# Ten blocks instead of eight by seven products, the division moved from VectorE to ScalarE and GpSimd, one turning for two, quarter sums behind the last slot

## Chip, cores, metric

The kernel runs on one core of one Trainium2 chip. The metric is the device time of one execution in microseconds (us). "The profile" is one execution recorded by the hardware profiler, "the trace" its single instructions. L followed by a number is a line of the kernel that the profile belongs to, so the same statement has different numbers in different kernels.

## The reference, cut to what matters

Threshold attention over 8 batches of 8 heads, 576 positions, head size 64; its output is the input x of an MLP with exact GELU.

```python
scores = scale * np.matmul(q, k.transpose(0, 1, 3, 2))
thresh = np.max(scores, axis=-1, keepdims=True) - tau
scores = np.where(scores >= thresh, scores, -1000000000.0)
attn = np.exp(scores - np.max(scores, axis=-1, keepdims=True))
attn = attn / (np.sum(attn, axis=-1, keepdims=True) + 1e-09)
x = attn @ v                       # to (4608, 512)
h = x @ w_in                       # 512 -> 2048
g = 0.5 * h * (1.0 + erf(h / sqrt(2)))
out = g @ w_out                    # 2048 -> 512
```

## The kernel before, the parts that matter

The 4608 rows of x are 18 blocks of 256. The first ten are "plain": their matmuls fill gaps of TensorE while attention runs. The last eight go two at a time ("duos") through an algorithm with seven products of quarters instead of eight, after attention. Attention goes by 32 pairs of heads with five slots each (four of 128 query rows, and the tails of both heads). From pair 4 on, p (the unnormalized attention) is turned by VectorE in 32x32 squares and regrouped by transfers from SBUF to SBUF into pT. In slot 2 of the next pair, TensorE makes xT = v^T pT, and it is divided by the row sums, which a series of transfers has laid out as inv.

```python
def softmax_head(p, i):                # per slot
    nc.vector.tensor_reduce(nmx, sc, op=ALU.max, negate=True)
    nc.gpsimd.tensor_scalar(thr, nmx, -1.0, tau_eff, ...)
    nc.scalar.activation(w, sc, AF.Exp, bias=nmx)
def softmax_tail(p, i):
    nc.vector.scalar_tensor_tensor(row, sc, thr, row, op0=ALU.is_ge, op1=ALU.mult, accum_out=den)
def divisors(p):                       # slot 4, behind the tail
    ...
    nc.sync.dma_start(rows, turned)    # to DRAM
    ...                                # four transfers back, spread over the partitions:
    nc.sync.dma_start(inv, rows)
def regroup(p, i):
    if i == 1:
        s["pT"] = [one.tile([P, KR, S], ...) for e in range(2)]   # pool of one buffer
    for a in range(4):
        ...                            # i = 1 (in slot 2) and i = 3: columns of two slots
        for e in (1, 0):
            nc.sync.dma_start(pT[e][:, :, a*P:(a+1)*P][:, :, half], pd[e][rows, :, half])
# order of one slot
scores; softmax_head; gelus of the slot before; (slot 2: xT); softmax_tail;
divide; turn_p; divide; regroup; divisors; next(loads of q, k or v on gpsimd); turn_qk; fill
```

In the traces of this case every engine, and every queue that issues transfers, goes through its instructions in the order of the program (below, thr of slot 3 starts 0.04 us after the last load of k ahead of it).

## Time and profile before

| | kernel before |
|---|---|
| time, median of the first 3 runs | 1431.48 us (1431.28 to 1433.82) |
| xT of pair 4 starts (the "first xT") | 206.6 us |
| from there to the 5th xT (four pairs) | 117.7 us |
| xT of the 5th to the 27th pair, period | 30.55 us (324.3 to 996.4 us, 22 periods) |
| last of these xT to the second duo | 88.2 us |
| one duo | 97.5 us |

The 28 pairs with turning are counted from pair 4 on. What follows the start of the second duo is three times 97.5 us (four times after) and a rest of 52.9 us that the change leaves nearly alone (52.6 after). So the rows add up to the span, and each change of time can be booked in one of them. The 22 periods are read from the starts of xT on TensorE.

### The profile page before, as it was taken

How to read it: one execution, taken by the hardware profiler on the slowest of the kernel's cores; microseconds unless marked ns; L12 is line 12 of the kernel's file. 1: busy time of each engine (PE TensorE's matmuls, PEld its weight loads, DVE VectorE, ACT ScalarE, POOL GpSimd, SP SyncE). 2: the span in 40 equal slices, each digit the busy share in tenths (PEclk: the TensorE clock that was granted, in tenths of full speed). 3: DMA queues.
4: the chain of work that ended last, by engine and by line, in shares of the span. 5: the costliest groups of instructions: out<-in, count | busy, mean ns of one | idle time of the engine just before them, and what ended most of it. 6: DMA issues, size and time to landing. Idle time of an engine off the chain costs nothing.

```text
span 1430.0 us, 19776 instructions
## 1 busy us (share of the span) xinstructions
PE 1385.1 (97%) x6544; PEld 960.9 (67%) x6544; DVE 900.0 (63%) x1908; ACT 640.8 (45%) x1039; POOL 389.1 (27%) x810
## 2 busy tenths in 40 slices
PE   5898999999999999999999999999999999999999
PEld 4666547566466574665746657466488888888887
DVE  5887787777767777777777777777654142241230
ACT  5758525436256373562745627457142141230320
POOL 4443244433434434434434344330000000000000
PEclk8999999999999999999999999999999999999999
DMA  9977167776667776677776777765500100100000
GB/s 260 297 264 241 40 144 150 152 150 133 131 137 145 153 147 133 142 140 159 156 140 143 160 154 152 142 135 100 107 0 1 44 1 0 59 1 8 22 1 30
DMA packets 449492, 167.06 MB, mean 117 GB/s; under 512 B 413040, under 2 KB 432048, under 8 KB 449392
## 3 DMA queue, kind: packets, MB, share of 16 engines
q1 hardware_dynamic: 423184, 108.65, 38.8%
q0 software_dynamic: 23808, 56.57, 12.9%
q8 instruction: 53, 0.87, 0.2%
q10 hardware_dynamic: 2400, 0.59, 0.2%
q14 instruction: 47, 0.39, 0.1%
HBM read 71.68 MB, written 11.47 MB: 58 GB/s over the span
## 4 chain that ended last, share of the span: by engine, by line
PE 85%; DVE 6%; ACT 5%; DMA 2%; issue 1%; SPq 1%; POOL 0%; DVEq 0%; ACTq 0%; POOLq 0%
PE bank L641 27%; PE hT L520 18%; PE o_ps L532 17%; PE sc L355 12%; PE xT L460 9%; ACT p L370 2%; DVE p L386 1%; PE tr L301 1%; DVE nmx L367 1%; DVE power L185 1%; ACT L500 1%; ACT diag L400 1%; DMA pd<-in_moe_w_in_dram 1%; ACT L507 0%; DVE expo L176 0%
## 5 line engine op out<-in xcount | busy, mean ns | idle before, releaser
L370 ACT ACTIVATE p<-sc,nmx 128x576 f32<-128x576 f32 x288 | 202.5, 739 | 384.4 <-DVE nmx L367 384.4
L367 DVE TENSOR_REDUCE nmx<-sc 128x1 f32<-128x576 f32 x288 | 205.0, 749 | 149.8 <-PE sc L355 149.8
L520 PE MATMUL hT<-x,w_in 128*128 128x256 f32 x1280 | 296.2, 384 | 0.0
L532 PE MATMUL o_ps<-w_out,g 128*128 128x512 f32 x640 | 295.1, 604 | 0.0
L520 PEld LDWEIGHTS hT<-x,w_in 128*128 128x128 f32 x1280 | 238.4, 190 | 56.9 <-issue 25.2
L386 DVE SCALAR_TENSOR_TENSOR p<-sc,thr,p 128x576 f32<-128x576 f32 x288 | 225.4, 816 | 65.2 <-ACT p L370 64.2
L368 POOL TENSOR_SCALAR thr<-nmx,tau_eff 128x1 f32<-128x1 f32 x288 | 85.0, 295 | 547.4 <-DVE nmx L367 544.9
L532 PEld LDWEIGHTS o_ps<-w_out,g 128*128 128x128 f32 x640 | 117.1, 190 | 141.0 <-issue 139.2
L355 PE MATMUL sc<-kT,qT 64*128 64x288 f32 x960 | 165.0, 432 | 2.6 <-DVE p L386 2.4
L460 PE MATMUL xT<-pT,v 128*64 128x288 f32 (+2 forms) x1280 | 164.4, 409 | 3.2 <-ACT g L500 3.2
L433 DVE STREAM_TRANSPOSE pd<-p 128x576 f32<-128x576 f32 x224 | 160.8, 756 | 2.9
L355 PEld LDWEIGHTS sc<-kT,qT 64*128 64x128 f32 x960 | 92.9, 187 | 84.2 <-issue 71.8
L460 PEld LDWEIGHTS xT<-pT,v 128*64 128x64 f32 x1280 | 90.2, 137 | 73.4 <-issue 13.5
L232 POOL DMA_DIRECT2D v<-in_v_dram x208 | 111.0, 537 | 10.5 <-issue 9.5
L641 PE MATMUL bank<-x,w_in 128*128 128x256 f32 x384 | 94.7, 383 | 3.2 <-DVE x L655 3.2
L507 ACT ACT_TABLE_LOAD x71 | 91.1, 1283 | 1.3
L500 ACT ACT_TABLE_LOAD x71 | 91.1, 1283 | 1.3
L641 PE MATMUL bank<-unit 128*128 128x256 f32 x352 | 88.6, 382 | 0.0
L641 PEld LDWEIGHTS bank<-x,w_in 128*128 128x128 f32 x384 | 73.7, 192 | 14.2 <-issue 4.1
L223 POOL DMA_DIRECT2D q<-in_q_dram x104 | 70.9, 686 | 15.9 <-issue 15.0
L641 PEld LDWEIGHTS bank<-unit 128*128 128x128 f32 x352 | 67.4, 192 | 9.4
L301 PE MATMUL tr<-diag,p 128*128 128x128 f32 (+1 forms) x360 | 51.8, 312 | 22.1 <-ACT diag L400 13.8
(143 smaller groups left out, 1346.4 us busy)
## 6 DMA issues: line engine op xcount, KB each, us to landing
pT<-pd SPq DMA_DIRECT2D x448, 160.0 KB, 3.9
pT<-pd_tail SPq DMA_DIRECT2D x112, 80.0 KB, 2.8
q<-in_q_dram POOLq DMA_DIRECT2D x104, 72.0 KB, 4.0
k<-in_k_dram POOLq DMA_DIRECT2D x104, 72.0 KB, 2.6
out_dram<-o_sb SPq DMA_DIRECT2D x28, 256.0 KB, 3.9
inv<-turned SPq DMA_DIRECT2D x56, 128.0 KB, 3.9
v<-in_v_dram POOLq DMA_DIRECT2D x156, 40.0 KB, 3.0
raw<-in_moe_w_in_dram POOLq DMA_DIRECT2D x8, 512.0 KB, 5.5
```

Of the source, the lines that this page charges most:

```text
L232: eng.dma_start(t[r:P:4, e, 0:n, :], rows[:, r * KR:r * KR + n, :])
L355: nc.tensor.matmul(sc[e][:, h, 0:HALF], lhsT=lhsT, rhs=s["kT"][rows, at:at + HALF], start=True, stop=True)
L367: nc.vector.tensor_reduce(nmx[:, e:e + 1], sc, axis=AXIS.XY, op=ALU.max, negate=True)
L370: nc.scalar.activation(w[:, e * S:(e + 1) * S].rearrange("p (h s) -> p h s", h=2), sc, AF.Exp, bias=nmx[:, e:e + 1], scale=1.0)
L386: nc.vector.scalar_tensor_tensor(row, sc[e][:, :, 0:HALF], thr[:, e:e + 1], row, op0=ALU.is_ge, op1=ALU.mult, accum_out=den[e])
L433: nc.vector.transpose(to[:, 0:NB, :], w[:, e * S:(e + 1) * S].rearrange("p (b i) -> p b i", i=Q))
L460: nc.tensor.matmul(xT[f, 0:hi - lo], lhsT=s["v"][:, e, c, :], rhs=pT[:, c, lo:hi], start=(c == 0), stop=(c == KR - 1))
L500: nc.scalar.activation(t, hT, AF.Gelu)
L507: nc.scalar.activation(warm[:, 1:2], warm[:, 0:1], AF.Exp)
L520: nc.tensor.matmul(hT[:, j % 2, :], lhsT=w_in_sb[c][:, j * P:(j + 1) * P], rhs=x_blk[n][:, c, :], start=(c == 0), stop=(c == N_DM - 1))
L532: nc.tensor.matmul(o[:, 0:d_model], lhsT=g[j][:, m * P:(m + 1) * P], rhs=w_out_sb[j], start=(j == 0), stop=(j == N_DF - 1))
L641: nc.tensor.matmul(to, lhsT=l, rhs=r, start=start and k == 0, stop=k == len(pairs) - 1, skip_group_check=not start)
```

## The change

Its intent: two more blocks by seven products save an eighth of their matmul work; the smaller fill then needs shorter slots, so VectorE is relieved (division by ScalarE and GpSimd, two turnings in one); the start and the turn to the last stage lose waits.

```diff
-    PLAIN = N_BLK - 8
+    PLAIN = N_BLK - 10
-    AWAY = [PLAIN, PLAIN + 1, PLAIN + 2]
+    AWAY = list(range(PLAIN, PLAIN + 5))
+    warm = const.tile([P, 2], FP32, name="warm")      # was allocated behind the weights
+    nc.vector.memset(warm, 0.0)
     ident = const.tile([P, P], FP32, name="ident")
...
-    pd = [const.tile([P, 4 * KR, P], FP32, name=f"pd{e}") for e in range(2)]
+    turned_p = const.tile([P, 2, 4 * KR, P], FP32, name="turned_p")
+    pd = [turned_p[:, e, :, :] for e in range(2)]
...
-        for e in reversed(range(n)):                   # two turnings of 576
-            nc.vector.transpose(to[:, 0:NB, :], w[:, e * S:(e + 1) * S]...)
+        nc.vector.transpose(turned_p[:, :, 0:NB, ...], w.rearrange(...))   # one of 1152
...
-                    nc.vector.tensor_tensor(to, x, by[:, at:at + size], op=ALU.mult)
+                nc.scalar.copy(to, x)
+                if by is not None:
+                    nc.gpsimd.tensor_tensor(to, to, by[:, at:at + size], op=ALU.mult)
...                                                     # seven-product stage
+        x_sums(x_ext, *DUOS[0])                         # in weights_in, behind the last slot
-                nc.sync.dma_start(out[row:row + P, :], hi[m])
+                store(n2, m, hi[m], 0)                  # half-width stores, earlier
...
+    nc.scalar.activation(warm[:, 1:2], warm[:, 0:1], AF.Exp)    # behind load_early(0)
-        convert(3000 if n < 2 * HP else ...)
+        convert(0 if n == 0 else 3400 if n < 2 * HP else ...)
```

The multiplies now stand where xT is made, ahead of the loads of k on GpSimd.

More of the change, by code (lines that the diff above doesn't have):

```diff
@@ L67 @@
     N_BLK = B * S // TOK
-    PLAIN = N_BLK - 8
-    AWAY = [PLAIN, PLAIN + 1, PLAIN + 2]
-    order = list(range(PLAIN + 3, N_BLK)) + AWAY
+    PLAIN = N_BLK - 10
+    AWAY = list(range(PLAIN, PLAIN + 5))
+    order = list(range(PLAIN + 5, N_BLK)) + AWAY
     DUOS = list(zip(order[0::2], order[1::2]))
@@ L429, in turn_p @@
         w = s.pop(("p", i))
-        n = 1 if i == NC else 2
-        for e in reversed(range(n)):
-            to = pd_tail[p % 2] if i == NC else pd[e][:, :, i * Q:(i + 1) * Q]
-            nc.vector.transpose(to[:, 0:NB, :], w[:, e * S:(e + 1) * S].rearrange("p (b i) -> p b i", i=Q))
+        if i == NC:
+            nc.vector.transpose(pd_tail[p % 2][:, 0:NB, :], w[:, 0:S].rearrange("p (b i) -> p b i", i=Q))
+            return
+        nc.vector.transpose(
+            turned_p[:, :, 0:NB, i * Q:(i + 1) * Q], w.rearrange("p (e b i) -> p e b i", e=2, i=Q))
     def regroup(p, i):
@@ L474, in divide @@
                 to, x = x_blk[n][:, hp, o:o + size], xT[:, at - lo:at - lo + size]
-                if by is None:
-                    nc.scalar.copy(to, x)
-                else:
-                    nc.vector.tensor_tensor(to, x, by[:, at:at + size], op=ALU.mult)
+                nc.scalar.copy(to, x)
+                if by is not None:
+                    nc.gpsimd.tensor_tensor(to, to, by[:, at:at + size], op=ALU.mult)
                 at += size
-        if by is not None:
-            return divide
         divide()
@@ L491 @@
     dirty = [False]
-    warm = const.tile([P, 2], FP32, name="warm")
-    nc.vector.memset(warm, 0.0)
     def gelus(left):
@@ L512, in block_steps @@
         g = {}
+        mlp["layer"] = 1
         for j in range(N_DF):
@@ L526, in block_steps @@
             for j in range(N_DF):
+                mlp["layer"] = 2
                 yield NS_OUT, len(pieces) - N_DF + j + 1
@@ L537, in block_steps @@
             nc.sync.dma_start(out[row:row + P, :], o_sb)
-    mlp = {"n": 0, "steps": None, "next": None, "debt": 0.0}
+    mlp = {"n": 0, "steps": None, "next": None, "debt": 0.0, "layer": 0}
     def fill(ns, tokens):
@@ L584, in weights_in @@
         room += unit(work, "p", 2) + unit(work, "p", 2)
-        rest = [units(v_sb[i % 4])[0] for i in range(NP - 4, NP - 1)]
+        x_ext = [units(v_sb[i % 4])[0].rearrange("p (c t) -> p c t", c=NK) for i in range(NP - 4, NP - 1)]
         s1, s2, s4 = ({} for _ in range(3))
@@ L594, in weights_in @@
                 vec.tensor_tensor(s4[c, h], w_in_sb[NK + c][:, lo], s2[c, h], op=ALU.subtract)
-        return (s1, s2, s4), room + rest
+        assert mlp["n"] == PLAIN and mlp["layer"] == 2
+        for h in range(HF // U):
+            for c in range(NK):
+                a = w_in_sb[c][:, HF + h * U:HF + (h + 1) * U]
+                vec.tensor_tensor(a, w_in_sb[c][:, h * U:(h + 1) * U], a, op=ALU.subtract)
+        x_sums(x_ext, *DUOS[0])
+        return (s1, s2, s4), x_ext, room
     away = {}
@@ L605, in bring, with x_sums, strassen @@
         nc.sync.dma_start(x_blk[n], away.pop(n))
-    def strassen(ext, room):
+    def x_sums(x_ext, n1, n2):
+        t1, t2, t4 = x_ext
+        a, b = x_blk[n1], x_blk[n2]
+        b11, b21, b12, b22 = a[:, 0:NK, :], a[:, NK:2 * NK, :], b[:, 0:NK, :], b[:, NK:2 * NK, :]
+        vec.tensor_tensor(t1, b12, b11, op=ALU.subtract)
+        vec.tensor_tensor(t2, b22, t1, op=ALU.subtract)
+        vec.tensor_tensor(b12, b22, b12, op=ALU.subtract)
+        vec.tensor_tensor(t4, b21, t2, op=ALU.subtract)
+    def strassen(ext, x_ext, room):
         s1, s2, s4 = ext
-        for h in range(HF // U):
-            for c in range(NK):
-                a = w_in_sb[c][:, HF + h * U:HF + (h + 1) * U]
-                vec.tensor_tensor(a, w_in_sb[c][:, h * U:(h + 1) * U], a, op=ALU.subtract)
         room = room + units(v_sb[(NP - 1) % 4]) + [u for t in pd_tail for u in units(t)]
         room += [x for _ in range(2) for x in unit(xg, "x", 2)]
-        x_ext = [room.pop().rearrange("p (c t) -> p c t", c=NK) for _ in range(3)]
         o_ext = [room.pop() for _ in range(2)]
@@ L647, in bank @@
             return ps.tile([P, 512], FP32, tag="mm", name="bank")
-        def x_sums(n1, n2):
-            t1, t2, t4 = x_ext
-            a, b = x_blk[n1], x_blk[n2]
-            b11, b21, b12, b22 = a[:, 0:NK, :], a[:, NK:2 * NK, :], b[:, 0:NK, :], b[:, NK:2 * NK, :]
-            vec.tensor_tensor(t1, b12, b11, op=ALU.subtract)
-            vec.tensor_tensor(t2, b22, t1, op=ALU.subtract)
-            vec.tensor_tensor(b12, b22, b12, op=ALU.subtract)
-            vec.tensor_tensor(t4, b21, t2, op=ALU.subtract)
         def w_out_sums(j):
@@ L664, in w_out_sums, with store @@
             vec.tensor_tensor(wt4(j), b21, wt2(j), op=ALU.subtract)
+        def store(n, m, t, at):
+            row = n * TOK + m * P
+            nc.sync.dma_start(out[row:row + P, at:at + HD], t[:, at:at + HD])
         def finish_chunk(j, x, p3):
@@ L671, in finish_chunk @@
             vec.tensor_tensor(g21(j), g11(j), g21(j), op=ALU.subtract)
-        x_sums(*DUOS[0])
         for sb, (n1, n2) in enumerate(DUOS):
@@ L724, in strassen @@
                 vec.tensor_tensor(lo[m][:, 0:HD], lo[m][:, 0:HD], vs[m], op=ALU.add)
+                store(n1, m, lo[m], 0)
             for n in DUOS[sb + 1] if sb + 1 < len(DUOS) else ():
@@ L728, in strassen @@
             if sb + 1 < len(DUOS):
-                x_sums(*DUOS[sb + 1])
+                x_sums(x_ext, *DUOS[sb + 1])
             for m in ms:
@@ L742, in strassen @@
                 vec.tensor_tensor(hi[m][:, HD:2 * HD], hi[m][:, HD:2 * HD], xs[m], op=ALU.add)
-                row = n2 * TOK + m * P
-                nc.sync.dma_start(out[row:row + P, :], hi[m])
+                store(n2, m, hi[m], HD)
             for m in ms:
@@ L747, in strassen @@
                 nc.scalar.copy(lo[m][:, HD:2 * HD], xs[m])
-                row = n1 * TOK + m * P
-                nc.sync.dma_start(out[row:row + P, :], lo[m])
+                store(n1, m, lo[m], HD)
     load_early(0)
+    nc.scalar.activation(warm[:, 1:2], warm[:, 0:1], AF.Exp)
     load_early(1)
@@ L769 @@
     GOAL = [(-1, 0.0), (START - 1, 0.0), (BATCH - 1, 0.55)]
-    GOAL += [(BATCH * (m + 2) + WEIGH, x) for m, x in enumerate([1.96, 3.3, 4.64, 5.98, 7.32, 8.66, PLAIN])]
+    GOAL += [(BATCH * (m + 2) + WEIGH, x) for m, x in enumerate([1.96, 2.97, 3.98, 4.98, 5.99, 6.99, PLAIN])]
     def goal(n):
@@ L796 @@
             table()
-        made = []
         for args in due:
@@ L801 @@
         if p > EARLY and i == WEIGH:
-            made = [weigh_v(p - 1, h * HALF, (h + 1) * HALF) for h in range(2)]
+            for h in range(2):
+                weigh_v(p - 1, h * HALF, (h + 1) * HALF)
         owed += (goal(n) - goal(n - 1)) * BLK_NS * (PARTS[i] if not early and p < NP else 1.0)
@@ L811 @@
             softmax_tail(p, i)
-        if made:
-            made[0]()
         if p < NP and not early:
             turn_p(p, i)
-        if made:
-            made[1]()
         if p < NP and not early:
@@ L845 @@
             turn_qk(p + 1)
-        convert(3000 if n < 2 * HP else 3650 if n < BATCH - 1 else 1e9)
+        convert(0 if n == 0 else 3400 if n < 2 * HP else 3650 if n < BATCH - 1 else 1e9)
         if early:
```

## The prediction

> **What bounds the kernel now.** I read the page first (busy shares, then the 40 slices), then the busy time by stretch, the chain that ended last, and the timeline of single slots.
>
> ```profile
> PE 1385.1 (97%) x6544; PEld 960.9 (67%) x6544; DVE 900.0 (63%) x1908; ACT 640.8 (45%) x1039; POOL 389.1 (27%) x810
> ...
> 0.00:40.00 40.00, 24.69 (x150) 18.79 (x150) 22.66 (x56) 23.19 (x49) 18.66 (x46) 0.87 0.97 269
> 560.00:600.00 40.00, 40.00 (x184) 25.01 (x182) 30.86 (x63) 15.86 (x22) 15.81 (x33) 1.00 0.72 147
> 1000.00:1040.00 40.00, 36.77 (x131) 19.19 (x128) 23.08 (x44) 5.70 (x9) 0.88 (x3) 0.92 0.48 95
> 1120.00:1160.00 40.00, 40.00 (x187) 35.19 (x186) 9.88 (x24) 12.12 (x31) 0.00 (x0) 1.00 0.12 40
> ```
>
> The columns are PE, PEld, DVE, ACT and POOL busy, granted clock, DMA share, GB/s. TensorE is full from 200 us on, except at the turn from attention to the seven-product stage near 1030 us; the start is two thirds full. In the middle stage VectorE is already 77% busy and DMA 72%: TensorE binds there only because plain MLP blocks fill it.
>
> ```profile
> 990.85 4.49 PE o_ps L532 x10
> 996.51 5.00 PE xT L460 x40
> ...
> 1182.21 96.97 PE bank L641 x448
> 1279.68 96.97 PE bank L641 x448
> ```
>
> These pieces of the chain give the prices. One duo (two blocks by seven products) starts every 1279.68 - 1182.21 = 97.5 us. A plain block has 128 instructions of L520 and 64 of L532; longer runs in the chain grow by 0.215 us and 0.43 us an instruction, so two blocks cost 2 x (128 x 0.215 + 64 x 0.43) = 110 us at the margin.
>
> The middle stage goes by pairs of heads, in five slots each: scores, softmax, turning, then fill. Starts of consecutive xT are 30.5 us apart on average (294.75 to 996.51 us, 23 pairs). One full slot:
>
> ```profile
> 594.29 1.24 PE L355 MATMUL sc<-kT,qT 64*128 64x288 f32 x8
> 595.46 4.58 PE L520 MATMUL hT<-x,w_in 128*128 128x256 f32 x20
> 595.57 1.42 DVE L367 TENSOR_REDUCE nmx<-sc 128x1 f32<-128x576 f32 x2 [1.24 <-PE sc L355]
> 596.36 1.41 ACT L370 ACTIVATE p<-sc,nmx 128x576 f32<-128x576 f32 x2 [4.53 <-DVE nmx L367]
> 597.20 0.82 DVE L386 SCALAR_TENSOR_TENSOR p<-sc,thr,p 128x576 f32<-128x576 f32 x1 [0.21 <-ACT p L370]
> ...
> 598.80 1.44 DVE L433 STREAM_TRANSPOSE pd<-p 128x576 f32<-128x576 f32 x2
> 599.98 1.24 PE L355 MATMUL sc<-kT,qT 64*128 64x288 f32 x8
> ```
>
> TensorE's slot is 599.98 - 594.29 = 5.7 us, of which 20 fill instructions are 4.5. VectorE's round, from maximum to the end of the turning, is 600.24 - 595.57 = 4.67 us: only 1 us of slack.
>
> **What the Trainium skill says.** (1) "GPSIMD Engine Reference", Elementwise: a two-input elementwise op takes about 2.6 cycles an element at 1.2 GHz, and the engine has no PSUM access. The latter is why ScalarE must copy first. No GpSimd multiply is in this trace; even its one-element thr takes 295 ns. (2) "ScalarE: Activation LUTs", What ACT_TABLE_LOAD costs: 1283 ns a load, which the page repeats exactly (1283). The section gives 186 ns + 0.833 ns an element for an ACTIVATE with immediate scale and bias; the trace's PSUM copy of 512 takes 584 ns. (3) "VectorE: DVE Perf Modes", Side-by-side: about 150 cycles of fixed cost an instruction; the turning of 576 takes 756 ns, 156 over 576/0.96. (4) "TensorE: Matmul & The Clock Gate", What's actually happening: an idle window near 3.4 us halves the clock. The trace agrees: after a 3.23 us wait, groups of four that later take 0.86 us take 1.7.
>
> **The change, part by part.**
>
> *Two blocks move.* The fill of the last 24 of the 28 pairs shrinks from 0.335 to 0.251 block (the first four keep theirs). The fifth duo adds 97.5 us for certain. What comes off depends on how far the pair can shrink; nominally 110, net -12.7.
>
> *TensorE's new pair.* A pair's fill in L520 instructions is 0.251 x 256 = 64, shared 1.2, 1.2, 0.8, 1.2, 0.6. A full slot: scores 1.17 + 15.4 x 0.215 + 0.17 for switching = 4.67 us. Slot 2: 1.17 + 5.0 (xT) + 10.3 x 0.215 + 0.17 = 8.56. Slot 4 is too short: 2.8 us of PE work, but the next scores wait for its L386, in this trace 3.65 us after slot 4's scores started. Sum 3 x 4.67 + 8.56 + 3.67 = 26.2; with the same arithmetic for before I get 30.4 (measured 30.5). So at best 24 x 4.2 = 101 us come off, not 110.
>
> *VectorE.* Divides leave it: 112 in all, some 1.2 us a pair, but in slot 2, where it has slack. One turning of 1152 instead of two of 576 is 156 + 1200 = 1.36 us for 1.44 (estimate): its round falls to 4.6, just under TensorE's 4.67. So both are needed merely not to make VectorE the bound.
>
> *ScalarE.* Four copies a pair, 4 x 186 + 576 x 0.833 = 1.2 us, estimated from that section. A slot with one gelu takes exp 1.41 + two loads 2.57 + gelu 0.60 + gaps, about 4.75 us: on the edge, near +0.1 a slot.
>
> *GpSimd.* Four multiplies a pair of 576 columns together: 576 x 2.17 ns + 4 x 0.25 = 2.2 us (estimate from the first section and the 295 ns of thr). What matters is their place in the queue, below.
>
> *Ends.* The quarter sums stand behind the last slot, before the last pair's division, so the 3.23 us wait below and the slow clock after it (2.6 us) should go; a new wait for the last pT may give back a bit: -5. Dropping the conversions in slot 0 keeps VectorE from waiting for weights at 18 to 21 us ahead of the second slot's maximum: -3 to -4. Early table load and half-width last stores: some tenths.
>
> ```profile
> 1034.57 2.04 PE L641 MATMUL bank<-x,w_in 128*128 128x256 f32 x4 [3.23 <-DVE x L655]
> ```
>
> **The rivals.** *A: TensorE stays the bound.* Pair 26.3 us with the ScalarE edge: 1431.5 + 97.5 - 24 x (30.5 - 26.3) - 9 = 1419 us. For it: the slots were plainly sized so that 4.67 meets 4.6.
>
> *B: GpSimd's queue becomes the wait.* In the changed order GpSimd runs, in slot 2: thr, four multiplies, four loads of k, then thr of slot 3. The multiplies need inv, which comes at the end of a long DMA series:
>
> ```profile
> 584.59 8.16 SPq L448 DMA_DIRECT2D pT<-pd  x8
> ...
> 599.60 0.60 SPq L419 DMA_DIRECT2D inv<-turned  x1
> ...
> 603.00 2.69 POOL L223 DMA_DIRECT2D k<-in_k_dram  x4
> ```
>
> The series starts as slot 3 is turned (584.59), and inv's second half is issued at 599.60 and lands 4.4 us later: 19.4 us, set by DMA and not shortened. In the kernel before that is 4 us into slot 2, just when VectorE is free to divide. In the changed one slot 2 begins 2.9 us earlier relative to the series, and the joint turning starts it 0.7 later: inv lands 7.6 us into slot 2. Then multiplies 2.2, loads of k 2.7, thr 0.3: 12.9 us into slot 2. L386 of slot 3 wants thr 8.5 + 1.28 + 1.64 = 11.4 us in. So it starts 1.4 us late, the scores of slot 4 wait on it, and nothing makes up for it: pair 27.7 us, total 1431.5 + 97.5 - 24 x 2.8 - 9 = 1453 us. For it: order and durations; against it: the multiply's duration is an estimate, and whoever sized the fill would have seen such a wait.
>
> *C: DMA binds.* From the end of xT, 20 transfers at about 1 us each plus landing 2.8 and xT's second half 2.5 make a loop of 25.8 us (the pT buffer is single), while loads of k now fall among the pT transfers. The mean share would rise from 72% to about 80%. If transfers stretch by a tenth, pair 28 to 28.5, total 1460 to 1472.
>
> *D: a full gain.* If slot 4 didn't wait and the ends gave more: 1405 to 1410.
>
> **Range and chances.** The loss of slots against the certain 97.5 us leaves little gain in any rival: only D comes near 2% (under 1403). I hold B a little likelier than A by its mechanism, and A likelier than it looks because the change appears tuned; between 1419 and 1453 I put 1438, with 1412 to 1464 to take in A and the milder half of C. Faster by over 2%: 0.05; within: 0.80; slower, over 1460: 0.15.
>
> **What would show it.** The duos: five of 97.5 us. Pairs of xT 26.2 to 26.5 us apart speak for A; about 27.7, with L386 waiting for thr some 1.4 us once a pair and a like wait of scores for L386 on TensorE, for B; SP issue without gaps and xT waiting for pT, for C. The turning: one op near 1.36 us. The multiplies: near 0.5 us each; much longer or much shorter breaks B's sum. The wait of 3.23 us gone and the clock at 1.00 at the turn; the second maximum near 17 us instead of 21.57. The prediction is wrong if pairs fall below 26 us (slot 4 did not hold them) or if the fifth duo is dearer than 97.5.

## More of the kernel before

The page and the slot are shown in the prediction. One view is added: the queue of SyncE (SPq), which issues pT, turned and inv. Columns: start, duration of the issues, queue, line, transfer and count; a gap between lines is time in which nothing is issued (a line of many issues can hide short gaps inside).

```profile
600.24 0.62 SPq L421 DMA_DIRECT2D inv<-turned  x1
606.29 16.82 SPq L448 DMA_DIRECT2D pT<-pd  x16
623.21 3.44 SPq L444 DMA_DIRECT2D pT<-pd_tail  x4
626.75 0.58 SPq L413 DMA_DIRECT2D turned<-turned  x1
```

Between the last inv (600.86 us) and the first pT (606.29) this queue stands 5.4 us: it waits for xT to have read the old pT. That gap is the slack of the kernel before.

## The result, and the profile after

| | before | after | difference |
|---|---|---|---|
| time, median of 4 | 1431.38 us (1428.93 to 1433.82) | 1500.91 us (1499.34 to 1505.41) | |
| span of the profiled run | 1430.0 us | 1499.4 us | +69.4 |
| first xT | 206.6 | 209.7 | +3.1 |
| four pairs | 117.7 | 117.5 | -0.2 |
| 22 periods of xT | 22 x 30.55 | 22 x 29.43 | -24.8 |
| last of these xT to the second duo | 88.2 | 82.2 | -6.0 |
| fifth duo | | 97.5 | +97.5 |

The ratio is 1.0491 (95% interval 1.0462 to 1.052). Ratios here are the mean time of one kernel's runs over that of the other's of the same rounds, so not quite the ratio of the medians. Only the fifth duo adds much, and the pairs give too little back: the shorter fill shortened the pair by 1.1 us where 2.8 (rival B) or 4.2 (rival A) was predicted. After, in the columns of the prediction's fences: the page's busy times, the busy times by stretch, and the chain at the turn.

```profile
PE 1398.0 (93%) x6608; PEld 983.1 (66%) x6608; DVE 895.5 (60%) x1750; ACT 650.3 (43%) x1166; POOL 438.2 (29%) x922
```

```profile
0.00:40.00 40.00, 25.02 (x136) 19.31 (x137) 19.02 (x48) 22.03 (x47) 16.12 (x41) 0.94 0.97 251
560.00:600.00 40.00, 35.64 (x198) 24.54 (x198) 29.35 (x53) 29.32 (x41) 17.89 (x37) 1.00 0.78 135
1120.00:1160.00 40.00, 39.49 (x183) 34.44 (x183) 16.43 (x41) 16.14 (x41) 0.00 (x0) 1.00 0.00 1
```

```profile
974.72 5.00 PE xT L464 x40
1056.92 96.97 PE bank L652 x448
```

From 560 to 600 us TensorE has 4.4 us of idle time, which it did not have before (40.00 busy); the start and the duos look as before, and the chain has the turn at 82.2 us. VectorE is busy for 29.35 of these 40 us, where it was 30.86 before, so its load alone isn't the bound. SyncE's queue after:

```profile
593.91 0.58 SPq L416 DMA_DIRECT2D turned<-turned  x1
597.72 0.60 SPq L422 DMA_DIRECT2D inv<-turned  x1
...
600.57 17.79 SPq L452 DMA_DIRECT2D pT<-turned_p  x16
618.45 3.62 SPq L448 DMA_DIRECT2D pT<-pd_tail  x4
622.17 0.58 SPq L416 DMA_DIRECT2D turned<-turned  x1
626.00 0.59 SPq L422 DMA_DIRECT2D inv<-turned  x1
...
628.74 7.82 SPq L452 DMA_DIRECT2D pT<-turned_p  x8
636.66 2.40 SPq L537 DMA_DIRECT2D out_dram<-o_sb  x1
```

The 5.4 us of slack are gone. Two pauses are left in a round: the 3.2 us from the end of turned's issue (622.75) to the first inv (626.00), in which turned lands in DRAM, and one that the line of 16 issues hides: its ninth issue starts at 610.51, 1.9 us after the eighth has ended, since slot 3 must be turned first. From turned to turned is 622.17 - 593.91 = 28.3 us. What this queue waited for from 330 to 975 us (total us, times, longest), two lines of the kernel before, then two of the changed one:

```profile
SPq L448 <- PE xT L460: 117.5, 22, 7.1
SPq L419 <- DMA turned<-turned: 28.3, 21, 1.5
```

```profile
SPq L422 <- DMA turned<-turned: 65.2, 23, 4.3
SPq L452 <- PE xT L464: 6.1, 6, 1.3
```

So the slack, the wait for xT, was used up in the whole stage, and at the same time the queue's own round grew: without its gap it took 30.5 - 5.4 = 25.1 us before. A store of a plain block, 2.40 us, stands in the same queue and comes on top. TensorE's xT ran from 595.43 to 600.50, and the next pT is issued at 600.57: that is a second round of the same length, xT 5.1, pT 17.8, tails 3.7, landing 1.4 until the next xT at 623.49. A third goes through GpSimd. These are lines of the chain that ended last in the same pair (start, duration, what):

```profile
627.30 3.72 DMA inv<-turned
...
631.87 1.14 POOL x L481 x3
...
634.34 1.32 POOL k L226 x2
...
635.70 0.32 POOL thr L371
...
636.78 0.83 DVE p L389 x3
...
637.64 1.38 DVE turned_p L436
```

inv lands, the multiplies run, then the loads of k, then thr of slot 3, then VectorE masks and turns slot 3, without which the second half of pT and the next turned can't go. The waits after, from 330 to 975 us (engine, line, releaser: total us, times, longest):

```profile
POOL x L481 <- DMA inv<-turned: 119.3, 17, 9.6
DVE p L389 <- POOL thr L371: 51.2, 29, 3.5
PE sc L358 <- DVE p L389: 43.5, 38, 2.6
```

Before, VectorE waited 0.6 us in all for thr in this stage. So three rounds met in one pair: GpSimd's queue, SyncE's queue, and the single buffer pT. The last two are 28.1 to 28.3 us long here; the length of the first alone isn't shown. The experiments take them apart.

### The profile page after: what moved, and what is told of

The parts are those of the page before. It is cut to its first block, busy times and chain, and to the rows that moved or that the text cites. A ratio compares the mean times of both kernels' runs of the same rounds, so it can differ in the third digit from the quotient of the medians. Undisturbed runs are those within 1.5% of the kernel's fastest.

```text
span 1499.4 us, 20084 instructions
## 1 busy us (share of the span) xinstructions
PE 1398.0 (93%) x6608; PEld 983.1 (66%) x6608; DVE 895.5 (60%) x1750; ACT 650.3 (43%) x1166; POOL 438.2 (29%) x922
## 4 chain that ended last, share of the span: by engine, by line
PE 52%; DVE 12%; DMA 12%; ACT 8%; POOL 6%; issue 5%; SPq 4%; DVEq 0%; POOLq 0%; ACTq 0%
PE bank L652 32%; PE sc L358 6%; PE hT L519 5%; PE o_ps L532 5%; DMA inv<-turned 5%; DMA turned<-turned 4%; DVE p L389 4%; ACT p L373 3%; POOL k L226 3%; DVE turned_p L436 3%; PE xT L464 3%; DVE nmx L370 2%; POOL x L481 2%; DMA pT<-turned_p 1%; ACT L505 1%
## 5 line engine op out<-in xcount | busy, mean ns | idle before, releaser
L519 PE MATMUL hT<-x,w_in 128*128 128x256 f32 x1024 | 244.0, 389 | 0.0
L532 PE MATMUL o_ps<-w_out,g 128*128 128x512 f32 x512 | 238.9, 605 | 0.0
L519 PEld LDWEIGHTS hT<-x,w_in 128*128 128x128 f32 x1024 | 192.1, 192 | 52.4 <-issue 24.7
L532 PEld LDWEIGHTS o_ps<-w_out,g 128*128 128x128 f32 x512 | 92.8, 190 | 110.4 <-issue 107.7
L436 DVE STREAM_TRANSPOSE turned_p<-p 128x1152 f32<-128x1152 f32 x112 | 154.4, 1378 | 4.9 <-DMA pT<-pd_tail 1.1
L652 PE MATMUL bank<-x,w_in 128*128 128x256 f32 x480 | 116.7, 379 | 0.0
L652 PE MATMUL bank<-w_out,unit 128*128 128x256 f32 x520 | 115.5, 379 | 0.0
L652 PEld LDWEIGHTS bank<-w_out,unit 128*128 128x128 f32 x520 | 98.8, 190 | 13.4
L481 POOL TENSOR_TENSOR x<-x,inv 128x192 f32<-128x192 f32 (+7 forms) x112 | 51.3, 490 | 186.6 <-DMA inv<-turned 157.8
L652 PE MATMUL bank<-v,unit 128*128 128x256 f32 x320 | 82.1, 379 | 0.0
```

The lines of the kernel that those rows point to most:

```text
L436: nc.vector.transpose(turned_p[:, :, 0:NB, i * Q:(i + 1) * Q], w.rearrange("p (e b i) -> p e b i", e=2, i=Q))
L519: nc.tensor.matmul(hT[:, j % 2, :], lhsT=w_in_sb[c][:, j * P:(j + 1) * P], rhs=x_blk[n][:, c, :], start=(c == 0), stop=(c == N_DM - 1))
L532: nc.tensor.matmul(o[:, 0:d_model], lhsT=g[j][:, m * P:(m + 1) * P], rhs=w_out_sb[j], start=(j == 0), stop=(j == N_DF - 1))
L652: nc.tensor.matmul(to, lhsT=l, rhs=r, start=start and k == 0, stop=k == len(pairs) - 1, skip_group_check=not start)
```

## The experiments

Eighteen kernels ran, all correct. "Pair" is the mean of the 22 periods, read as above. The kernel before took 1428.3 to 1429.9 us (medians) beside them.

### Which part costs: div_dve, eight, ten

div_dve puts the old division back into the changed kernel; eight is the changed kernel with eight seven-product blocks; ten is the kernel before with ten.

```diff
 # div_dve
-                nc.scalar.copy(to, x)
-                    nc.gpsimd.tensor_tensor(to, to, by[:, at:at + size], op=ALU.mult)
+                    nc.vector.tensor_tensor(to, x, by[:, at:at + size], op=ALU.mult)
 # eight (ten is the reverse, in the kernel before; AWAY and the goals of the fill go with it)
-    PLAIN = N_BLK - 10
+    PLAIN = N_BLK - 8
```

> The changed kernel, with the division back on VectorE straight out of the accumulator, as before the change (no copies by ScalarE, no multiplies by GpSimd); ten blocks, joint turning and all else kept. Theory 1 (queue of GpSimd): VectorE now takes the wait for inv itself, in slot 2, but GpSimd is free: pair 27.5 to 28.5, time 1450 to 1478 us. Theory 2 (series of transfers): pair 29 or more, time above 1488 us. Theory 3 (VectorE's own work is the bound): the pair becomes longer than 29.4, time above 1505 us.

> The changed kernel with eight blocks by seven products and the old fill, all else kept. If the new engine placement costs only where the fill is too small to hide it (theories 1 and 2 alike), the pair stays at 30.5 us and the time is 1424 to 1440 us (6 us from the turn gained, 3 at the start lost). If the waits cost in full whatever the fill, since they stop the scores that stand ahead of the fill, the pair is 31.5 us or more and the time above 1455 us.

> The kernel before with ten blocks by seven products and the smaller fill, all else as before (divide on VectorE, two turnings, quarter sums behind the last division). Theory 1: VectorE's round and the divide set the pair, 28 to 28.5 us, time about 1428 + 97 - 24 x 2.3 = 1470 us. Theory 2 (series of transfers): pair 29.4, time 1500 us or more. If it were the old engine placement that bounds, and the new one had helped, it would be slower than the changed kernel, above 1505 us.

| run | time | ratio to before | pair |
|---|---|---|---|
| div_dve | 1511.62 us | 1.0586 | 30.05 |
| eight | 1435.21 us | 1.0049 | 30.66 |
| ten | 1481.41 us | 1.0374 | 28.82 |

eight: with the old fill the new placement costs the pairs 0.1 us; the waits hide, and the time is in its first range. ten, whose time fell between its two theories: the move of two blocks alone loses 53 us (1481.41 - 1428.33), with not one instruction moved between engines, so GpSimd's multiplies can't be the root. In ten it is VectorE that waits for inv (55.3 us in 18 places from 330 to 975 us, longest 6.9). div_dve against after (1500.91): the move of the division as such gains 10.7 us. By the ratios to the kernel before it gains 14. div_dve's pair and time are above the limits of its theories 2 and 3 alike; but ten has the same division on VectorE and even one turning more in a slot, and its pair is shorter, so VectorE's own work (theory 3) doesn't set 30.05 us. That div_dve is 30 us slower than ten was open at this point.

### Taking GpSimd's queue away: defer

```diff
-                    nc.gpsimd.tensor_tensor(to, to, by[:, at:at + size], op=ALU.mult)
+                    held.append((to, by[:, at:at + size]))
             softmax_head(p, i)
+            if i == WEIGH + 1:
+                multiply()            # the held multiplies, behind thr of slot 3
```

(Left out: the last pair multiplies in slot 2, and fill from a finished batch and the putting away of its x come one slot later, since x is complete later.)

> The changed kernel, with the four GpSimd multiplies of a pair issued behind the thr of slot 3 instead of ahead of the loads of k in slot 2 (nothing else). Theory 1 (the queue of GpSimd: the wait for inv holds back thr, thr holds the masking on VectorE, that holds the scores): the waits of VectorE for thr (54.6 us in 31 places) and of TensorE for VectorE's masking (43 us) nearly vanish, the pair falls from 29.4 to between 26.5 and 28 us, the time to 1430 to 1466 us. Theory 2 (the series of transfers pT, turned, inv, pT sets the pair, and the wait for inv is only where it shows): the pair stays at 29 us or more, the time above 1488 us, and the waits move to TensorE waiting for pT.

Measured: 1494.85 us, ratio 1.046, pair 29.17. Its waits over the same stretch:

```profile
DVE p L395 <- POOL thr L377: 7.7, 13, 0.9
PE xT L470 <- DMA pT<-pd_tail: 18.5, 8, 4.7
```

The wait for thr fell from 51.2 to 7.7 us, and the time by 6 us only, at the edge of what the intervals tell apart (1.0427 to 1.0493 here, 1.0462 to 1.052 for the changed kernel): another wait stands in its place, xT for pT. Theory 1 (rival B) as the single cause fell.

### Fewer, wider transfers: wide, defer_wide

```diff
-            half = slice((i - 1) * Q, (i + 1) * Q)
+            if i == 1:
+                continue
-                nc.sync.dma_start(...[:, :, half], pd[e][rows, :, half])
+                nc.sync.dma_start(s["pT"][e][:, :, a * P:(a + 1) * P], pd[e][rows])
```

> The changed kernel with the regrouping of p after slot 3 alone, in 8 transfers of 128 columns instead of 8 of 64 after slot 2 and 8 of 64 after slot 3 (the same bytes, half as many pieces, and no transfer waits for the end of xT any more). All else kept, the multiplies too. Theory 2 (loop of xT end, 17.8 us of pT transfers, 3.7 of tails, 1.4 of landing, xT 5.1 us: 28.1 us, on SyncE's queue also with turned and inv) says that this loop goes, and GpSimd's queue is left: pair 27 to 28 us instead of 29.4, time 1445 to 1470 us. Theory 1 (GpSimd's queue alone) says that nothing changes: 1495 to 1510 us. If the later start of the transfers costs more than the fewer pieces save, it is slower than 1510 us, with TensorE waiting for pT.

> Both: multiplies behind the thr of slot 3 as in the run before (1494.9 us), and 8 wide transfers. If the two waits are two parallel bounds, each covering the other, taking both away gives what neither gives alone: pair 26.3 to 27 us and 1425 to 1445 us. If one of them alone were the cause, this equals the better of the two single edits within 5 us.

Measured: 1816.28 and 1819.13 us. Both failed: the whole regrouping now stands behind slot 3, and is not short enough.

```profile
602.93 13.94 SPq L453 DMA_DIRECT2D pT<-turned_p  x8
616.97 5.10 SPq L448 DMA_DIRECT2D pT<-pd_tail  x4
...
644.18 13.36 SPq L453 DMA_DIRECT2D pT<-turned_p  x8
```

Eight issues of 320 KB stretch over 13.4 to 13.9 us; sixteen of 160 KB stretched over 17.8, of which 15.3 were issues and the rest pauses. Whether the width is why isn't shown: SyncE's packets also took only 45.1% of the 16 engines' time from 330 to 920 us, for 70.6% in the changed kernel. But 41 us pass from one series to the next, since nothing is moved in slots 2 and 3 any more: the third case of wide's expectation. These runs say only that the start of the series matters more than the size of its pieces; they tell nothing about GpSimd.

### Two turnings again: two_turns, ten_joint

```diff
 # two_turns, in the changed kernel (two buffers pd again); ten_joint is the reverse, in ten
-        nc.vector.transpose(turned_p[:, :, 0:NB, ...], w.rearrange(...))
+        for e in (1, 0):
+            nc.vector.transpose(pd[e][:, 0:NB, i * Q:(i + 1) * Q], w[:, e * S:(e + 1) * S]...)
```

> The changed kernel with two turnings of 576 instead of one of 1152 (two buffers again, as before), all else kept. The kernel before with ten blocks alone took 1481 us, the changed kernel with the old division 1511 us; the joint turning is the largest difference left between these. If the joint turning is what costs (transfers that wait for a later end of turning, or one buffer for both heads), time 1475 to 1485 us. If it doesn't matter, 1500 us, within 5.

> The kernel before with ten blocks (1481.4 us) and, beyond that, the joint turning of both heads in one buffer; nothing else. If the joint turning is why the changed kernel with the old division took 1512 us, this takes 1500 to 1515 us. If it is harmless (taking it out of the changed kernel gained only 6 us, 1501 to 1495), 1478 to 1488 us, and the rest stays with the start and what the other phase of the transfers does.

two_turns: 1494.9 us, ratio 1.0458, pair 29.17 (after: 29.43). ten_joint: 1492.53 us, ratio 1.0439, pair 29.21 (ten: 28.82). The joint turning doesn't gain; it costs some 6 to 11 us (the intervals of ten and ten_joint lie apart, those of two_turns and the changed kernel overlap). It was expected to be either harmless or the whole difference, and is neither. Why it costs isn't shown: VectorE itself saves 0.06 us a slot.

### Opening the rounds one by one: defer_inv, once, free_pt, free_pt_out

```diff
 # defer_inv: defer, and inv issued by GpSimd in slot 2 instead of by SyncE
-            nc.sync.dma_start(to[:, 0:MAIN]..., src)
+            nc.gpsimd.dma_start(to[:, 0:MAIN]..., src)
 # once: the buffer is taken from its pool once and kept
-            s["pT"] = [one.tile([P, KR, S], ...) for e in range(2)]
+            if not late_pT:
+                late_pT.extend(one.tile([P, KR, S], ...) for e in range(2))
+            s["pT"] = late_pT
 # free_pt: defer_inv and once.  free_pt_out: and the stores leave SyncE's queue
-            nc.sync.dma_start(out[row:row + P, :], o_sb)
+            nc.scalar.dma_start(out[row:row + P, :], o_sb)
-        nc.sync.dma_start(away[n], x_blk.pop(n))
+        nc.gpsimd.dma_start(away[n], x_blk.pop(n))
```

> Multiplies behind the thr of slot 3, and the four transfers of inv issued by GpSimd in slot 2 instead of by SyncE behind turned. Theory 2a (SyncE's queue in order: the wait of some 3 us for turned to land and the four inv hold back the next pT): pair 26.5 to 27.5 us, time 1430 to 1455 us. Theory 2b (the loop over the single pT buffer and the end of xT, for which inv is no matter): no gain, 1488 to 1500 us.

> The changed kernel with the buffer pT taken from its pool once and kept, instead of taken anew for each pair; nothing else. Then a transfer into it needs to wait only for the matmuls that read the same columns (the first half of xT), not for the whole of xT. In the changed kernel two series meet within 0.3 us: xT's end to the next pT, and SyncE's own queue (16 pT 17.8, 4 tails 3.7, turned 0.6, wait 3.2, 4 inv 2.5: 27.8 us and any store in that queue on top). Theory 2 with both: freeing one alone gains little, 1490 to 1500 us. If the pT buffer alone were the bound: pair 27 us, 1450 us or less. If neither (GpSimd's queue): 1501.

> Multiplies behind the thr of slot 3, inv issued by GpSimd (as in the run before, 1484.1 us), and pT kept: all three series opened. Theory 2 (series on SyncE and the single pT buffer): pair 26.8 to 27.5 us, time 1445 to 1465 us. If the amount of DMA work bounds (engines 85% busy, pieces of 256 bytes slower than before), no gain over 1484 us: 1478 to 1488.

> As the run with all three opened, and the ten stores of plain blocks and five stores of set-aside x in this stretch leave SyncE's queue (the stores are issued by ScalarE, which makes the data, and the set-aside by GpSimd). Those pairs in which such a store stands took 30 to 34 us against 27 for the others. Theory 2: all pairs near 26.8 us, time 1430 to 1450 us. If the amount of DMA work bounds, those pairs stay long: less than 8 us gained by this edit.

| run | opened | time | ratio | pair |
|---|---|---|---|---|
| after | nothing | 1500.91 us | 1.0491 | 29.43 |
| defer | GpSimd's queue | 1494.85 us | 1.046 | 29.17 |
| once | pT buffer | 1494.67 us | 1.0445 | 29.23 |
| defer_inv | GpSimd's and SyncE's queues | 1484.11 us | 1.0381 | 28.57 |
| free_pt | all three | 1458.25 us | 1.0193 | 27.69 |
| free_pt_out | and the stores moved | 1452.66 us | 1.0153 | 27.28 |

GpSimd's queue or the pT buffer opened alone gains 6 us; GpSimd's and SyncE's queues together 17; all three 43. SyncE's queue alone was not run. The buffer gains 6 us on the changed kernel and 26 on defer_inv (1484.11 - 1458.25). That is what parallel bounds of nearly equal length look like: taking away one uncovers the next. defer_inv fell between its two theories, 29 us above the one's range and 4 below the other's. free_pt fell in the range of theory 2 (1445 to 1465). free_pt_out gained 5.6 us, less than the 8 that its theory asked for, and ended 2.7 us above its range: the stores count for less than said. What is left there may be the amount of transfers, as its rival has it: the mean DMA share from 330 to 950 us is 0.91, where it was 0.84 in the changed kernel and 0.71 before (330 to 970 us). That is not settled.

Two lines of SyncE's queue in free_pt, then one of TensorE, show what keeping the buffer does:

```profile
599.57 0.58 SPq L422 DMA_DIRECT2D turned<-turned  x1
604.05 9.52 SPq L468 DMA_DIRECT2D pT<-turned_p  x8
```

```profile
601.36 5.07 PE L480 MATMUL xT<-pT,v 128*64 128x288 f32 x40
```

The first pT is issued at 604.05, in the middle of xT (601.36 to 606.43), as soon as the first of xT's two halves is done. In the kernel before and after it waits for the end of both, since a buffer taken anew from a pool of one waits for all readers of the old one.

### The start: eight_start, eight_conv, free_start

```diff
 # eight_start: eight, and
-    nc.scalar.activation(warm[:, 1:2], warm[:, 0:1], AF.Exp)
-        convert(0 if n == 0 else 3400 if n < 2 * HP else ...)
+        convert(3000 if n < 2 * HP else ...)
 # eight_conv: eight, and only the line of convert.  free_start: free_pt_out and both
```

> The changed kernel with eight blocks (1435.2 us in its run) and the start of the kernel before: conversions of weights in slot 0 again, 3000 ns a slot, no warming Exp ahead of the second load. First xT stood at 209.1 to 210.4 us in the changed kernel's traces, at 202.7 and 206.6 in the kernel's before. If the start is what is lost: 1427 to 1431 us. With the 6 us of the turn it should come out at 0.995 to 1.000 of the kernel before. If the start isn't the cause: 1435.

> The changed kernel with eight blocks and only the conversions of the start as before (3000 ns a slot from slot 0); the warming Exp ahead of the second load stays. Both halves undone took 1428.0 us, none undone 1435.2 us. If the conversions are what loses: 1428 to 1430. If the Exp, which stands on ScalarE's queue ahead of the loads of k of the second pair, loses: 1433 to 1436. I hold the conversions likelier, since a delay of the k loads by 1.2 us can hardly grow to 7.

> The best of the ten-block versions (all three series opened, stores off SyncE's queue, 1452.7 us) with the start of the kernel before: 7 us less as in the eight-block pair of runs, 1444 to 1448 us. Still slower than the kernel before by over 1%: ten blocks do not pay at a pair of 27.3 us.

Measured: eight_start 1428.04 us (ratio 0.9983, interval 0.9966 to 0.9999), eight_conv 1428.63 us (0.9999, 0.9984 to 1.0014), free_start 1447.15 us (1.0125). eight was at 1.0049. So the later conversions lose some 7 us, and the warming Exp nothing that could be seen. free_start hit its range; the best ten-block version is still 1.25% slower than the kernel before.

### The ends alone, and a packet that takes longer: ends_only, aligned, ends_aligned

ends_only keeps of the change only the quarter sums behind the last slot and the half-width stores.

> Of the change only the two ends in the seven-product stage: quarter sums behind the last slot and stores of half width; eight blocks, old division, two turnings, old start. The wait of 3.2 us and the slower clock after it at the turn go (6 us in the changed kernel's trace), the pairs are untouched: 1422 to 1425 us, a ratio of 0.9945 to 0.997. If the earlier quarter sums delay the last pair's division, 1428 us and more.

Measured: 1428.48 us, ratio 0.9997 (0.998 to 1.0014): a miss. The turn did gain (last of the 22 xT to the second duo: 83.0 us for 88.2), but the pairs lost as much, 30.76 us for 30.55, though their instructions are the same. The view of transfers from 330 to 920 us gives SyncE's queue as packets, MB, and the time of its packets as a share of 16 engines; first the kernel before, then ends_only, then the changed kernel:

```profile
q1 hardware_dynamic: 275254, 68.02, 60.2%
```

```profile
q1 hardware_dynamic: 273201, 67.50, 64.0%
```

```profile
q1 hardware_dynamic: 284080, 70.48, 70.6%
```

Share x 16 x 590 us / packets is 20.65 ns a packet before, 22.11 in ends_only, 23.46 after. By the same sum ten has 20.92 and ten_joint 20.93, and every other kernel built on the changed one (wide, with its wider packets, aside) 22.7 to 24.1. These are means: the median 256-byte packet of this queue takes 18 ns in the kernel before, in ends_only and in the changed kernel alike, and the longer ones become more frequent (90% are within 33, 41 and 41 ns). What ends_only shares with the changed kernel in this stretch, and ten does not, is the place of one small tile: warm is allocated first instead of behind the weights. In the compiled programs, all constants behind it start 32 bytes further on: the source of the pT transfers at 29312 bytes before (458 x 64) and at 29344 after (32 over a multiple of 64), that of the tails at 50048 (782 x 64) and 50080. pT itself lies at 149600 in both.

```diff
 # aligned: the changed kernel, and; ends_aligned: ends_only, and
-    warm = const.tile([P, 2], FP32, name="warm")      # ahead of ident
-    nc.vector.memset(warm, 0.0)
+    warm = const.tile([P, 2], FP32, name="warm")      # behind w_out_sb
+    nc.vector.memset(warm, 0.0)
```

> The changed kernel with the tile of the warming Exp allocated behind the weights, as before, instead of first; nothing else (the warming Exp stays where it is). If the shift of the buffers by 32 bytes makes transfers slower: packets of SyncE's queue fall from 23.5 to about 21 ns, the 16 pT transfers from 17.8 to about 16.5 us, the pair by 0.8 to 1.5 us, and the time from 1501 to 1468 to 1485 us. If the place doesn't matter: 23 ns or more, 1498 to 1505 us.

> Only the quarter sums behind the last slot and the half-width stores, with every buffer of the middle stage where the kernel before has it. ends_only (1428.5, ratio 0.9997) lost in its pairs the 5 us that it gained at the turn. If the place of the buffers is why: packets 20.7 ns, pairs as before, 1423 to 1425 us, ratio 0.995 to 0.997, which would be the fastest of all. If not: 1428 to 1429 us again.

Measured: aligned 1483.63 us, ratio 1.038, pair 28.61; ends_aligned 1422.97 us, ratio 0.9948 (0.9935 to 0.996), pair 30.55. Their queue, aligned first:

```profile
q1 hardware_dynamic: 290735, 72.24, 68.5%
```

```profile
q1 hardware_dynamic: 276634, 68.36, 60.5%
```

That is 22.24 ns a packet in aligned and 20.65 in ends_aligned. The place of an 8-byte tile cost the changed kernel 17 us. Between ends_only and ends_aligned the engines' instructions take the same (a matmul of hT 383.5 ns in both), while an issue of pT takes 971 ns on average against 906; so it is the transfers that the place slows. But all constants moved by the same 32 bytes, and only two places were tried: which tile's place counts, and whether 64 is the step that matters, isn't shown. ends_aligned differs from ends_only in nothing else, repeats all 22 periods of the kernel before within 0.1 us, and is the fastest kernel of all, half a per cent under the kernel before. aligned's packets fell by half of what was expected (22.24, not 21): the other half stays with the changed kernel's order of work. That its loads of k now run beside pT is a likely reason, not a shown one. No kernel with all rounds opened and aligned was run; free_start would have to come down by 17.5 us (1447.15 - 1429.67) to meet the kernel before, so whether ten blocks can pay stays open.

## Why the prediction was wrong, point by point

- *The fifth duo, 97.5 us for certain*: right (97.5).
- *The turn, -5*: right; -6.0 in the changed kernel, and the 3.23 us wait is gone.
- *The start, -3 to -4*: wrong in sign. The second maximum did come earlier (19.34 us for 21.57, predicted 17), but the first xT came 3.1 us later in these two traces; eight_conv shows some 7 us for the conversions. The step ended at the first slot: it asked who waits for the conversions in slot 0, and not who needs their results later.
- *One turning, 1.36 us*: right in size (1378 ns), but two_turns and ten_joint show that it costs 6 to 11 us. The copies took 0.88 us a pair for 1.2, the multiplies 1.83 for 2.2.
- *Rival A, slots of 4.67 us*: the price of a slot was right. Slot 1 takes 4.63 us after, and slot 3 takes 4.54 in free_pt_out. Slot 2 and slots 4 and 0 together stay 0.6 us each above the sum even there (9.18 for 8.56, 8.92 for 8.34), so A's pair of 26.2 us was not to be had: 27.28.
- *Rival B, GpSimd's queue*: the mechanism is there as told: in the pairs where it stands, thr comes up to 3.5 us late (1.4 predicted). But B took a pair to be over with that wait. It treated inv's series as fixed (19.4 us, "set by DMA and not shortened"; 20.5 in the pair shown, 610.51 to 631.02 us) and moved the rest against it. In truth the late masking delays the turning of slot 3, so the second half of pT, so the next turned: the wait feeds the series that causes it, as the chain shows. Taking B away alone gained 6 us.
- *Rival C, the loop of DMA, 25.8 us* is the step that failed. It is the term that set the time, together with B, and it was sized too short (its terms as written make 25.3 us, not 25.8): I let xT's second half alone (2.5 us) stand in it, where the pool holds the buffer until both halves are done (5.1); I took 20 transfers at about 1 us each, where sixteen and four took 17.8 and 3.6; only the landing was shorter (1.4 for 2.8). And I left out that turned, its landing, inv and the stores pass through the same queue. Worked out from the trace as above the buffer's loop is 28.1 us and the queue's 28.3, and stores come on top; even C's upper estimate, a pair of 28.5 us, was short of the 29.43 measured. Part of it was visible in the kernel before: with the whole of xT the buffer's loop is there 5.1 + 20.4 and 1.4 to 2.8 for the landing, 27 to 28 us. The other part was not: the queue's round, 25.1 us there without its gap, left room for a pair of 26.2, but grew by 3.2 us, 1.8 of them in the time from turned to the first inv (2.0 us before, 3.8 after) and 1.1 in pT and tails. C had allowed for such growth ("If transfers stretch by a tenth"), but on a loop that was too short. Why turned lands later isn't shown.
- *What no step had*: the 32 bytes. The diff shows the moved allocation, and I read it as the warming of a table. It is worth 17 us of the 63 by which the prediction missed (1500.9 - 1438).
- The booking: two blocks moved, +53 (ten); joint turning +11 (ten_joint); 32 bytes +17 (aligned); conversions +7 (eight_conv); division moved -11 (after against div_dve); ends -7 (ends_aligned). From 1428 this gives 1498, and 1500.9 was measured, so the parts nearly add (each is a difference of medians, uncertain by some 3 us, and each was measured in one kernel only: by two_turns the joint turning is 6, not 11). If they add, they also make up the 30 us between ten and div_dve: 11 + 17 + 7 - 7 = 28.

## What to carry to other kernels

When a change is to shorten a period, make the sum of every queue and every single buffer around that period first, with what shares the queue; the slack that the profile shows there, not the busy share of any engine, is the most that can be taken off, and less where the round itself grows (here 5.4 us of slack stood in the queue, its round grew by 3.2, and the pair fell by 1.1). If taking a wait away gains little, look for the next round of equal length before giving the theory up. And compare the addresses of buffers that transfers read when a diff touches the order of allocations, even for eight bytes.

## What the Trainium skill lacked or had wrong

- "SBUF — State Buffer", Operand start alignment, says that its measurements are "about legality, not speed". Here speed depends on the place: with all constants 32 bytes further on, packets of the same program take 22.11 ns for 20.65 on average (ends_only against ends_aligned), and the changed kernel takes 1500.9 us for 1483.6. "DMA: Bandwidth & Descriptors", How a descriptor splits into AXI transactions, does say that a descriptor which does not start on a multiple of 256 bytes fetches unused bytes that cost time; the 256-byte rows of pT start off such a multiple in both places here (128 or 160 bytes past it), and no run tries one on it. No page gives a time for it.
- "DMA: Bandwidth & Descriptors", Issuing engines are not separate DMA queues, says that issuing from several engines saves only the sequencer's issue time, usually small. Here a wait for a landing stands in the in-order queue as well (65.2 us in 23 places ahead of inv, 2.8 on average), and sixteen issues with their pauses stretch over 17.8 of 28.3 us; moving inv to another engine took 10.7 us off (1494.85 to 1484.11).
